# Strip attention on one Trainium2 core: eleven VectorE units in 14 of the 28 pairs instead of 21, and a new written-out order

## The chip, the core and the metric

The kernel runs on one core of one Trainium2 chip. A core has five engines that run their own instruction streams and meet only at semaphores: TensorE (PE; its weight loads are shown apart as PEld), VectorE (DVE), ScalarE (ACT), GpSimd (POOL) and SyncE (SP, which here only issues DMAs). The metric is device time in microseconds (us), smaller is better. Times of several runs are given as the median with the lowest and the highest; the profile is one further execution, with a time of its own.

## What is computed

A projection to q, k and v, attention inside strips, and an output projection, for an image of 224 x 224 tokens with 96 channels. The first 48 channels attend inside horizontal strips of 8 rows, the last 48 inside vertical strips of 8 columns; each strip has 8 x 224 = 1792 tokens.

```python
def reference(x, wqkv, wo):
    B, H, W, C = x.shape
    sw = 8
    C2 = C // 2
    nh, nw = (H // sw, W // sw)
    qkv = jnp.einsum('bhwc,cd->bhwd', x, wqkv)
    q, k, v = (qkv[..., :C].copy(), qkv[..., C:2 * C].copy(), qkv[..., 2 * C:].copy())
    scale = C2 ** (-0.5)
    qh = q[..., :C2].reshape(B * nh, sw * W, C2)
...
    ah = _softmax(jnp.einsum('bqc,bkc->bqk', qh, kh) * scale, axis=-1)
    oh = jnp.einsum('bqk,bkc->bqc', ah, vh).reshape(B, H, W, C2)
...
    return jnp.einsum('bhwc,cd->bhwd', o, wo)
```

## The kernel before

**Pairs, chunks and units.** 28 horizontal and 28 vertical strips are worked in pairs of two neighbours, `P` = 0 to 27: 0 to 13 are horizontal, 14 to 27 vertical. The 1792 queries of a pair come in four chunks (`CH`: 512, 512, 512 and 256). Keys come in 14 tiles of 128. One *unit* is 1024 columns of scores of the pair: a chunk of 512 queries against one tile of keys, for both strips, or the chunk of 256 queries against two tiles. So a pair has 14 + 14 + 14 + 7 = 49 units, and the kernel 1372.

**What a unit costs each engine.** PE makes the scores into two banks of PSUM (`qk_op`, L1015: 48 rows deep, the two strips in two row halves of the array). Then the exponential is taken, in one of two ways:

- on ACT (`add_a`, L1037): one ACTIVATE with Exp of 128 x 1024 from PSUM into a `PT` buffer; then PE makes one product with the values (`pv_op`, L968, 64 columns wide, the two strips in two column halves).
- on VectorE (`add_d`): L1075 reads the scores from PSUM and writes them as 16-bit integers, shifted so that the bits are a number's exponent and mantissa; L1088 and L1090 mask out mantissa (`U_sb`) and exponent (`E_sb`); L1094 multiplies I by U (`G_sb`). exp is E + G, and PE adds the two by making **two** value products. Two VectorE units share one L1088 and one L1090 of 2048 columns; an odd last unit of a pair has its own, of 1024 columns. The product of L1094 is made on POOL in two halves of 512, or on VectorE as one of 1024, as `PLAN["far"]` says (1 is POOL).

How many units of each chunk go to VectorE is in `NDC` and `NDP` (L25 to L30): 11 of 49 for pairs in `NDP`, 10 for the others. Before, `NDP` holds the 21 pairs with `P % 4 != 1`, so 21 x 11 + 7 x 10 = 301 units are VectorE's and 1071 are ACT's.

**Other work.** For the next pair, `prep` has PE make q, k (L686) and v (L761), VectorE move them out of PSUM (L700, L706, L766), and POOL centre k (L720, L724, L725). For a finished chunk VectorE copies the sums out (L931), PE applies `wo` (L809 for horizontal, L843 for vertical pairs, L847 at the end), and VectorE divides by the sum of the row (L796, L816, L853); in vertical pairs POOL adds the horizontal half (L859), and SP stores the result (L887).

**What sets the order.** The order is written out: `PLAN["pe"]`, `["dve"]` and `["pool"]` have one digit for each operation of these engines, in order, and the digit names the queue from which the next one is taken (`forced`). In `"pe"`, 1 and 2 are scores for ACT and for VectorE, 3 and 4 are value products of VectorE's and of ACT's units, 5 is the output projection, 6 the projections, 0 the start. In `"dve"`, 1 is L931, 2 is L1075, 3 the other moves out of PSUM, 4 is L1088, L1090 and L1094. ACT takes its exponentials one after the other in the order of the units. `PLAN["bank"]` gives the PSUM bank of each PE operation that opens one; a score result takes two of the eight. All engines run their streams strictly in that order, each instruction behind the semaphores of what it needs.

**Modes of PE.** Scores (L1015) and the vertical output projection (L843) use the array split by rows; all the rest uses it whole or split by columns. `SWITCH` in the planner charges each change between the two.

Of the kernel before, what the change touches and what calls it, by code (L numbers as in the profile page):

```python
# [25 lines left out]
NDP = {P: [3, 3, 3, 2] for P in range(28) if P % 4 != 1}  # L26


def ndc(P, c):
# [5 lines left out]
        "00000000000000000066611216162164144116444216331216431241641231431643441163446141541234133164412164412144312314"  # L35
        "31631451431244144126143153121433146124153341143444131235144123414414126413311463643164154134143163124614412614"
        "31145444134124163135164123135412144414412433112344144116344416312351431241641134445312416411463344144121543123"
        "14611364451231441163441233154113444412614412416312513411433444146123153114634413351541241634124136144123144116"
        "34434134124136134125144412316411463441213341146354154164144123133412314412414412316341163444135123164135414124"
        "41441461231634124133113644413312541441231641146344124313411634312441341261441231341441233144114644512316433153"  # L40
        "12416412314313411644431154444416415431531361241544123164114634114453341541231641241634125144144124133114434412"
        "54144113336412461441164431245143126134114533441414612351331241641146343124414411363412531441134464126134125144"
        "12413313412341541441163533416124415312461341144431163444412134412416313361441241541241631146441132331544113444"
        "12641441261331231341145444415412316311463433125144123164114534412341641146334144125413413312416441241641136441"
        "12444133113644312416441215431341241344123144164133123161331146345124153411444412361341134444615415416431313512"
        "44164123164114344412316311453441264134125144144124313312514414414611363354131254144123413416412416411463343141"
        "45124416313412416341241461113443344125144412133316412164412415411433334154124146134126133411634412441544121633"
        "11433544144164123154123146311446341241441164333125144113644512314314412441441612313412361341153444126133411263"
        "41441153444123416411463431333124154124163411264414411534441163354123164145123134412144414613312414312316441231"
        "44146135135312414414412613331163441144464451441331631241534124164114634114433441251344114644126314412514414123"  # L50
        "13412315411344436131641253144124163413514412416411463334143123146124134114644441214461133344125143411442154136"
        "12316412313313414412415441136446133125413124415411364441231544114634413313316441261341241641231441641144334125"
        "41341441231341241541241641146333134415413124414126133123154113644412315441146334154164144412613312316312464144"
        "11644341241334114634124415412415313613412413314364411444412531213314412313414313441241541163344143123154123154"
        "41146346114644611444463134151244415412316412416314412416411333441251344141153344412513341441241341241543164133"
        "14416412316312461441146443123144116336415312415314124413416412416412416412313313415441146341253134123154114464"
        "31244136144115343341431631241631241644126134114644412413311464441231334151244154124164124133113464431152344131"
        "34125134414412313415411463344154164164123163312416313464144126144144123153312414414412315312416411463331344164"
        "31441246144125144313412414414414615312361331231541136444412415411464441133644311344431531241531241641231641146"
        "44412413314441251334141125313341123444136144125144411463331463134125144412416411444334121641163363151244154124"  # L60
        "16312414316412164411433431231541144434415123315441231541144344123416411463341441246144121633113343412416441116"
        "36336124154124153124164134146124133124134134144415412415311633631541264431441254144134114334413441261331446121"
        "63414441231441126413311463441241541241531231614612431431331444144125143123314414412315441115336346113444641541"
        "64146163313613412414412614411344441231534124154124164114644412313412133411464441133633124415412315411344431251"
        "44411433441541241421316311366334166144164123134124144124154123153411466441313412441441231334154124153114444451"
        "312351331144444123313411434412541331241544113444124314311443152334154114421433114431433151534414445"),
    "dve": (
        "00000000000000000333333332332344323232443233313443432323244123443234323321342444133234423233333344133232333414"
        "23334323442322144313233244333233441323323333244312344323232344431323343133332342432344143232332344123443333332"
        "42421234413332344342333232144323323443214442323442424133321333244233344333331333233234431333323234243324124331"  # L70
        "32344323323344133323323444231323443323233244412334333132332443332144323233234431234432323244431333234312332344"
        "33233314423323234432144323423432412443123333244332344333333313323234412333234432321443233133323443232333413342"
        "32324431423443232324443134332312344323323344331323323443231233344234423321234431323234434323344132332323443313"
        "33234423442332124423133334423233443333132332344312333234421233244331332334432332334413232443231234432333234442"
        "41233431323323344323344413332323244314234423233234441344423132323344323344333313232323443214432332333444423144"
        "21244442343233441323323333334431333233234423231442313334234423233441343232334442133333423443232323444123343123"
        "32334443234441333323232344321444323323323214434441323234443233443331333234233442312344232332344344132314234442"
        "33332332334132334344441333233232344321444213323444323233443132332344432133333233244323234441233441332332344432"
        "34413232344432313332332334423324444412332313333323442344413423332444213234432332332334444421214423323333344333"
        "33333132234412332332344421234443132332344323441334232343333343242123323344334424412332313443432334442414423323"  # L80
        "34442144332343424444143333133333"),
    "pool": (
        "00000000022222221212122222222222222222112122222222222222221212122222222222222222221112222222222222222222211122"
        "22222222222222222121212222222222222222221212122222222222222222212112222222222222222222221212122222222222222222"
        "21212122222222222222222221112222222222222222222121212222222222222222222121212222222222222222222212121222222222"
        "22222222212121222222223223222232222121213222233332222322222121212222233322332232222333112122222222233223322331"
        "21213222232222332222121213222222333223222221211322222222333322222213131322223332222322222233321212123223222233"
        "2222222121212332232222223333221311222222332222222222212121232233332232222222222313112233322223333322333333"),
    "far": (
        "11111011110111111101111111111111111011111111110111011111111111111111101111111111111111111111111101111111111111"  # L90
        "11110111111111111111110111111111111111111111111110111011101100111111110010010111111010101101111001110111010111"
        "011110101100110110110111101101110111011100101101111111101011111011010100001000000"),
    "bank": (
        "76547012376502064256045260426402640264026046207420742047024702470240642053053205203520346034604163416416431463"
        "12356135375073057305730460247024602460406240640635046240260426013601376024072407240720420742706420462042604620"
        "43026402640261356035063503603650361356135631573173510357124571351753153153023520375137512642651365135713602460"
# [1127 lines left out]
```

## Time and profile before

| | before |
|---|---|
| median of 3 runs, us | 1007.16 (1005.09 to 1011.97) |
| profiled execution, us | 1004.3, of which its span is 1002.5 |
| granted TensorE clock | 0.999 |
| busy share PE, ACT, DVE, POOL | 99%, 99%, 94%, 68% |
| Exp ACTIVATEs on ACT | 1071 |
| L1075 on VectorE | 301 |
| L1094 on POOL, halves / on VectorE, whole | 482 / 60 |

In the profile a line names line of the program, engine, operation and tiles, then the count, busy time, mean length of one, and the idle time of the engine ahead of them with what ended it. Records of consecutive instructions of one engine can overlap, because an engine starts the next while the last is still draining; so the mean length of one is more than the distance from one start to the next, and a busy share of 99% doesn't say that an engine never waits: a short wait can vanish under the overlap. For ACT the distance between starts is the better measure.

### The profile page before, as it was taken

How to read it: one execution, taken by the hardware profiler on the slowest of the kernel's cores; microseconds unless marked ns; L12 is line 12 of the kernel's file. 1: busy time of each engine (PE TensorE's matmuls, PEld its weight loads, DVE VectorE, ACT ScalarE, POOL GpSimd, SP SyncE). 2: the span in 40 equal slices, each digit the busy share in tenths (PEclk: the TensorE clock that was granted, in tenths of full speed). 3: DMA queues.
4: the chain of work that ended last, by engine and by line, in shares of the span. 5: the costliest groups of instructions: out<-in, count | busy, mean ns of one | idle time of the engine just before them, and what ended most of it. 6: DMA issues, size and time to landing. Idle time of an engine off the chain costs nothing.

```text
span 1002.5 us, 24560 instructions
## 1 busy us (share of the span) xinstructions
PE 988.0 (99%) x10211; PEld 385.9 (38%) x10211; DVE 938.5 (94%) x1573; ACT 987.6 (99%) x1080; POOL 684.2 (68%) x660
## 2 busy tenths in 40 slices
PE   8999999999999999999999999999999999999997
PEld 3433433343343334334334333433433443343342
DVE  8999999999999999999899999999999999999997
ACT  7999999999999999999999999999999999999997
POOL 3676766667677676777776776776676777677652
PEclk9999999999999999999999999999999999999999
DMA  5102120220112023011111122222122221222012
GB/s 110 39 2 38 38 32 8 38 38 1 39 39 32 8 38 38 2 36 25 27 29 32 25 46 50 54 52 44 34 41 52 53 54 39 52 52 40 13 36 50
DMA packets 164712, 36.92 MB, mean 37 GB/s; under 512 B 164488, under 2 KB 164488, under 8 KB 164600
## 3 DMA queue, kind: packets, MB, share of 16 engines
q1 hardware_dynamic: 163016, 34.80, 18.5%
q8 instruction: 80, 1.31, 0.5%
q10 hardware_dynamic: 1584, 0.55, 0.2%
q14 instruction: 32, 0.26, 0.1%
HBM read 0.44 MB, written 9.63 MB: 10 GB/s over the span
## 4 chain that ended last, share of the span: by engine, by line
ACT 70%; PE 29%; DVE 1%; issue 0%
ACT PT L1037 70%; PE ps L968 13%; PE ps L1015 11%; PE ps L686 2%; PE ps L761 1%; PE ps L843 1%; PE ps L532 0%; PE ps L809 0%; DVE OT_sb L931 0%; PE ps L647 0%; DVE out_sb L866 0%; DVE I_sb L1075 0%; DVE E_sb L1090 0%; DVE U_sb L1088 0%; PE ps L679 0%
## 5 line engine op out<-in xcount | busy, mean ns | idle before, releaser
L1037 ACT ACTIVATE PT<-ps 128x1024 bf16<-128x1024 f32 x1071 | 983.5, 1119 | 2.9 <-PE ps L1015 1.5
L1094 POOL TENSOR_TENSOR G_sb<-I_sb,U_sb 128x512 bf16<-128x512 bf16 x482 | 544.0, 1153 | 250.7 <-DVE E_sb L1090 225.3
L1015 PE MATMUL ps<-QT_sb,KT_sb 48*128 48x512 bf16 (+1 forms) x3136 | 463.0, 356 | 4.7 <-ACT PT L1037 3.0
L1075 DVE TENSOR_SCALAR I_sb<-ps 128x1024 int16<-128x1024 f32 x301 | 367.3, 1220 | 24.6 <-PE ps L1015 21.1
L968 PE MATMUL ps<-PT,V_sb 128*64 128x512 bf16 (+1 forms) x2422 | 363.8, 363 | 1.1 <-ACT PT L1037 1.0
L1015 PEld LDWEIGHTS ps<-QT_sb,KT_sb 48*128 48x128 bf16 x3136 | 123.2, 93 | 307.4 <-ACT PT L1037 223.7
L968 PEld LDWEIGHTS ps<-PT,V_sb 128*64 128x64 bf16 x2422 | 119.2, 109 | 122.5 <-issue 94.9
L968 PE MATMUL ps<-G_sb,V_sb 128*64 128x512 bf16 (+1 forms) x714 | 115.6, 356 | 0.0
L968 PE MATMUL ps<-E_sb,V_sb 128*64 128x512 bf16 (+1 forms) x714 | 109.9, 356 | 0.6 <-DVE OT_sb L931 0.2
L1088 DVE TENSOR_SCALAR U_sb<-I_sb 128x2048 int16<-128x2048 int16 (+1 forms) x161 | 109.2, 678 | 0.2
L859 POOL TENSOR_TENSOR out_sb<-tmp,Ph_sb 128x480 bf16<-128x480 f32 (+1 forms) x84 | 84.9, 1026 | 30.0 <-DVE E_sb L1090 10.7
L1090 DVE TENSOR_SCALAR E_sb<-I_sb 128x2048 int16<-128x2048 int16 (+1 forms) x161 | 104.9, 652 | 0.2 <-PE ps L968 0.2
L686 PE MATMUL ps<-xT_sb,w_sb 96*64 96x512 bf16 (+1 forms) x444 | 77.6, 367 | 0.9 <-ACT PT L1037 0.5
L931 DVE CAST OT_sb<-ps 128x512 bf16<-128x512 f32 x112 | 69.3, 619 | 5.9 <-PE ps L968 5.0
L706 DVE TENSOR_SCALAR_CACHE_REDUCE KT_sb<-ps 128x512 bf16<-128x512 f32 x110 | 67.8, 620 | 7.4 <-PE ps L686 6.8
L700 DVE TENSOR_SCALAR QT_sb<-ps 128x512 bf16<-128x512 f32 (+1 forms) x111 | 68.1, 619 | 5.2 <-PE ps L686 4.1
L766 DVE CAST V_sb<-ps 128x480 bf16<-128x480 f32 (+2 forms) x85 | 51.7, 611 | 3.1 <-PE ps L761 2.8
L968 PEld LDWEIGHTS ps<-G_sb,V_sb 128*64 128x64 bf16 x714 | 36.4, 108 | 47.3 <-issue 28.8
L720 POOL TENSOR_SCALAR KT_sb<-KT_sb,negmean 128x1792 bf16<-128x1792 bf16 x27 | 47.5, 1759 | 10.3 <-DVE E_sb L1090 6.2
L816 DVE TENSOR_TENSOR Ph_sb<-ps,rc 128x480 bf16<-128x480 f32 (+1 forms) x84 | 52.2, 622 | 2.1
L853 DVE TENSOR_TENSOR tmp<-ps,rc 128x480 f32<-128x480 f32 (+1 forms) x84 | 51.9, 618 | 2.2
L968 PEld LDWEIGHTS ps<-E_sb,V_sb 128*64 128x64 bf16 x714 | 33.9, 108 | 43.1 <-issue 21.1
(47 smaller groups left out, 324.4 us busy)
## 6 DMA issues: line engine op xcount, KB each, us to landing
out_dram<-out_sb SPq DMA_DIRECT2D x208, 42.0 KB, 2.1
xT_sb<-in_x_dram SPq DMA_TRANSPOSE x251, 2.4
out_dram<-out_sb SPq DMA_DIRECT2D x22, 24.0 KB, 1.9
Ph_sb<-in_x_dram ACTq DMA_DIRECT2D x1, 336.0 KB, 3.0
out_dram<-out_sb ACTq DMA_DIRECT2D x6, 24.0 KB, 1.9
wo_sb<-in_wo_dram SPq DMA_DIRECT2D x4, 9.0 KB
wo_sb<-one_sb SPq DMA_DIRECT2D x4, 0.0 KB
w_sb<-in_wqkv_dram ACTq DMA_DIRECT2D x1, 54.0 KB, 4.6
```

The lines of the kernel that those rows point to most:

```text
L686: ins = e.matmul(bk[64 * w:64 * w + 64, 0:qs], lhsT=w_sb[0:C, wblk(P, kind), :], rhs=rhs, start=True, stop=True)
L700: return e.tensor_scalar(dst, src, QS, None, ALU.mult)
L706: return e.tensor_scalar(dst, src, 1.0, None, ALU.mult, ALU.add, accum_out=acc)
L859: return e.tensor_tensor(out_sb[b][:, k0:k0 + nk, ws[0], :], t, Ph_sb[:, k0:k0 + nk, j0 + ws[0], :], ALU.add)
L931: return e.tensor_copy(OT_sb[b][:, q0:q0 + qs], bk[:, 0:qs])
L968: return e.matmul(bank(k.bank)[64 * w:64 * w + 64, x0:x1], lhsT=lhs(w, kts[i])[p0:p1], rhs=rhs(w, i, qs)[p0:p1, x0:x1], start=(op.tok["fir ...
L1015: ins = e.matmul(bank(op.tok["s"][w])[:, i * qs:(i + 1) * qs], lhsT=KT_sb[b][64 * w:64 * w + C2, kt * 128:(kt + 1) * 128], rhs=QT_sb[b][64 ...
L1037: a.fn = lambda e: e.activation(PT[a.tok["p"]][:].rearrange("p (s n) -> p s n", s=2), two(q.tok["s"]), ACTF.Exp, scale=LN128)
L1075: return e.tensor_scalar(dst[:, at:at + 1024].rearrange("p (s n) -> p s n", s=2), two(src), 128.0 * ONE, 0.0, ALU.add, ALU.max)
L1088: f.fn = lambda e: e.tensor_scalar(U_sb[y()][:, 0:m], I_sb[y()][:, 0:m], M_FRAC, HALF, ALU.bitwise_and, ALU.bitwise_or)
L1090: x2.fn = lambda e: e.tensor_scalar(E_sb[x2.tok["l"]][:, 0:m], I_sb[y()][:, 0:m], M_EXP, E_LOW, ALU.bitwise_and, ALU.bitwise_or)
L1094: g.fn = lambda e: e.tensor_tensor(G_sb[x2.tok["l"]][:, i0:i1], I_sb[y()][:, i0:i1].bitcast(BF16), U_sb[y()][:, i0:i1].bitcast(BF16), ALU. ...
```

## The change

`NDP` now holds the 14 odd pairs. Pairs 0, 2, 4, ... 26 have 10 units on VectorE (in 4, 2, 2 and 2 of their chunks), the odd pairs 11 (3, 3, 3 and 2). Pairs with `P % 4` of 0 or 2 lose one unit to ACT (14 pairs), pairs with `P % 4` of 1 win one from it (7 pairs); those with 3 stay. In all 14 x 11 + 14 x 10 = 294 units are VectorE's and 1078 ACT's. The five written-out lists are all replaced by others:

```diff
-NDP = {P: [3, 3, 3, 2] for P in range(28) if P % 4 != 1}
+NDP = {P: [3, 3, 3, 2] for P in range(1,28,2)}
...
 PLAN = {
     "pe": (
-        "00000000000000000066611216162164144116444216331216431241641231431643441163446141541234133164412164412144312314"
...
+        "00000000000000000066111626162161441164444216331126431441261344144163136144123144614613412415413314612234141441"
...
     "far": (
-        "11111011110111111101111111111111111011111111110111011111111111111111101111111111111111111111111101111111111111"
...
+        "11111110111101111111111111111111101111111111111111111011111111111111111111111110111111111111110111111111111111"
```

What stands in the lists, counted:

| | before | after |
|---|---|---|
| scores for ACT / for VectorE in `"pe"` (1 / 2) | 1071 / 301 | 1078 / 294 |
| value products for ACT's / VectorE's units (4 / 3) | 1071 / 602 | 1078 / 588 |
| projections, output projections (6, 5) | 277, 169 | 277, 169 |
| changes of PE's mode, into rows and out of them together | 1783 | 1837 |
| L1088 and L1090 of 2048 / of 1024 columns, each | 140 / 21 | 140 / 14 |
| L1094 on POOL in halves / on VectorE | 482 / 60 | 482 / 53 |

The shapes of all instructions, the buffers, the DMAs and the code that follows the lists are the same. The order on PE, VectorE and POOL differs from the first pair on; ACT's order is the same but for seven more exponentials, and SP issues the same transfers with stores and loads interleaved a little differently. The last pair (27) has the same split as before.

More of the change, by code (lines that the diff above doesn't have):

```diff
@@ L39 @@
[L39 to L48, printed above, removed]
@@ new lines @@
+        "13463316412451441231341441233135124164134114463312541431241544113443124416411463334133161245134124164412613411"
+        "44446133154123164124135134412414414612413312331441146344124161233136154123154441331144446414116345441544131631"
+        "23514412316441163441143344125413411464412631441251441421313412315441134436135146412315412416341341412641441143"
+        "33441361531461231441246134124146144112335134114446412613312514412441331133444124154146412316133312614414451231"
+        "33114644415441631241441136334125144114634441164344133154124163114544412613412414413341241541231454113443163124"
@@ L112 @@
+        "54204620274027402740274074207542052045204520452450250725072450250270502506270627062706240624060246052602560256"
+        "056250620604270624042604024602303570350370350350173416416413461476040"),
 }
```

125 lines of the change are left out of this document (64 added, 61 removed).

## The prediction

> **What bounds the kernel now.** I read the page from the top: the busy shares, then the chain of waits, then the groups, and then I cut the span at the borders of the pairs.
>
> ```profile
> span 1002.5 us, 24560 instructions
> ...
> PE 988.0 (99%) x10211; PEld 385.9 (38%) x10211; DVE 938.5 (94%) x1573; ACT 987.6 (99%) x1080; POOL 684.2 (68%) x660
> ...
> ACT 70%; PE 29%; DVE 1%; issue 0%
> ...
> L1037 ACT ACTIVATE PT<-ps 128x1024 bf16<-128x1024 f32 x1071 | 983.5, 1119 | 2.9 <-PE ps L1015 1.5
> ```
>
> PE and ACT are both at 99%, and the chain that ended last runs over ACT for 70% of the span and over PE for 29%. ACT's share is one kind of instruction, the exponential of a unit, 1071 times. Visible idle time ahead of it is 2.9 us. The mean record of 1119 ns is no price: records overlap. The price is the distance between starts, and the view of one line's instructions gives the first and the last start:
>
> ```profile
> L1037 ACT ACTIVATE PT<-ps x1071: 1018/1116/1300, 9.9 to 994.4; 128x1024 bf16<-128x1024 f32 x179
> ...
>   PEld ps L1015: 223.7, 696
> ```
>
> (994.4 - 9.9) / 1070 steps = 0.920 us for one. The last row says who waited for the exponentials: 696 times PE stood with the weights of the next scores until ACT gave a bank back. So mostly PE, with its work at hand, is paced by ACT; where the chain changes to PE, it is the other way.
>
> The trace of before already holds both kinds of pair that the change trades in. Here are stretches from the first exponential of a pair to the first of the next one, busy time by engine: first seven pairs with 10 VectorE units and 39 exponentials (first, two others and sum), then nineteen with 11 units and 38 (the quickest, the three longest, and the sum; pairs 0 and 27 are left out for start and end). The counts in brackets take in one or two exponentials that run across a border.
>
> ```profile
> 45.24:81.48 36.24, 36.23 (x394) 14.19 (x392) 33.05 (x56) 36.08 (x40) 22.92 (x23) 1.00 0.21 40
> ...
> 607.28:643.55 36.27, 35.69 (x366) 14.71 (x363) 34.47 (x57) 35.84 (x40) 25.51 (x25) 1.00 0.29 58
> 748.97:784.61 35.64, 35.64 (x362) 14.24 (x361) 34.28 (x58) 35.64 (x40) 24.61 (x24) 1.00 0.26 52
> ...
> sum 251.18, PE 249.97 PEld 99.45 DVE 231.91 ACT 250.40 POOL 174.04; mean PE 35.71 PEld 14.21 DVE 33.13 ACT 35.77 POOL 24.86
> ```
>
> ```profile
> 537.23:571.94 34.71, 34.71 (x350) 13.84 (x350) 33.24 (x56) 34.71 (x39) 24.93 (x25) 1.00 0.13 27
> 571.94:607.28 35.34, 34.90 (x350) 13.78 (x348) 34.16 (x58) 35.18 (x39) 25.37 (x25) 1.00 0.23 46
> ...
> 713.30:748.97 35.67, 35.47 (x360) 13.83 (x355) 35.10 (x60) 35.13 (x39) 23.53 (x23) 1.00 0.23 46
> ...
> 854.36:889.82 35.46, 35.19 (x350) 13.47 (x348) 34.36 (x58) 35.12 (x39) 24.88 (x24) 1.00 0.27 54
> ...
> sum 664.13, PE 660.48 PEld 255.50 DVE 631.02 ACT 663.09 POOL 472.06; mean PE 34.76 PEld 13.45 DVE 33.21 ACT 34.90 POOL 24.85
> ```
>
> A pair of 39 takes 251.18 / 7 = 35.88 us, one of 38 takes 664.13 / 19 = 34.95: 0.920 us an exponential in both, so a pair is as long as its exponentials. The spread inside a kind (34.71 to 35.67) is what the order and the neighbours do; the longest of this kind are pairs 16, 20 and 24, where VectorE is busy for 97 to 98% of the stretch.
>
> **The change, part by part.**
>
> *ACT gets seven more exponentials.* A pair that goes from 38 to 39 is 35.88 - 34.95 = 0.93 us longer, one that goes back is as much shorter. Fourteen go one way, seven the other: 7 x 0.93 = **+6.5 us**. Nothing can hide it: ACT has no gap from 9.9 to 994.4 us into which they would fit (2.9 us of idle time in all).
>
> *VectorE loses seven whole units.* Rows of the operations that go:
>
> ```profile
> L1075 DVE TENSOR_SCALAR I_sb<-ps 128x1024 int16<-128x1024 f32 x301 | 367.3, 1220 | 24.6 <-PE ps L1015 21.1
> L1094 DVE TENSOR_TENSOR G_sb<-I_sb,U_sb 128x1024 bf16<-128x1024 bf16 x60 | 41.9, 707 | 0.1
> L1088 DVE TENSOR_SCALAR U_sb<-I_sb 128x1024 int16<-128x1024 int16 x21 | 9.3, 441 | 0.0
> L1090 DVE TENSOR_SCALAR E_sb<-I_sb 128x1024 int16<-128x1024 int16 x21 | 8.8, 419 | 0.0
> ```
>
> Per unit 1.220 + 0.441 + 0.419 + 0.707 = 2.79 us, for seven 19.5 us (the products on POOL stay 482, so those that go are VectorE's own). VectorE has 1% of the chain, so this is off the path: at nothing by itself. But it is what the three long pairs want, and 16, 20 and 24 are among those that lose a unit. The other sixteen of their kind take (664.13 - 106.47) / 16 = 34.85, so the three are 106.47 - 3 x 34.85 = 1.9 us too long. Against that, pairs 1 and 17, the two long ones of the other kind (36.24 and 36.27), now win a VectorE unit. I take half of it: **-1.0 us**; bounds 0 and -1.9.
>
> *PE loses seven value products and gains 54 changes of mode.* PE's steps can be read from a stretch of its timeline (start, length, instruction):
>
> ```profile
> 300.48 0.60 PE L968 MATMUL ps<-PT,V_sb 128*64 128x512 bf16 x4
> 301.01 0.61 PE L1015 MATMUL ps<-QT_sb,KT_sb 48*128 48x512 bf16 x4
> 301.55 0.41 PE L968 MATMUL ps<-E_sb,V_sb 128*64 128x512 bf16 x2
> 301.79 0.38 PE L968 MATMUL ps<-PT,V_sb 128*64 128x512 bf16 x2
> 302.11 0.39 PE L1015 MATMUL ps<-QT_sb,KT_sb 48*128 48x512 bf16 x2
> 302.43 0.41 PE L686 MATMUL ps<-xT_sb,w_sb 96*64 96x256 bf16 x4
> ```
>
> Two matmuls run side by side as one step. From a value product to the next in the same mode it is 301.79 - 301.55 = 0.24 us; from one to scores, 302.11 - 301.79 = 0.32; from scores back, 302.43 - 302.11 = 0.32; four scores take 301.55 - 301.01 = 0.54, so a step inside the mode is 0.22. A change of mode costs 0.08 to 0.10 us. The lists have 1783 changes before and 1837 after: 54 x 0.09 = +4.9, less 7 x 0.22 = 1.5 for the products, so PE's own work grows by 3.4 us. This is paid where PE sets the pace, by the chain 29% of the time, and covered by its waits for ACT elsewhere: 0.29 x 3.4 = **+1.0 us**; bounds 0, if all lies in those 223.7 us of waits, and +3.4, if that cover is gone.
>
> [...]
>
> *Start and end.* Pair 27 is split as before, and the end (8.1 us from the last start to the span's end, 1002.5 - 994.4) has the same chain. Pair 0 has four VectorE units in its first chunk instead of three; by the spread of single pairs above, up to 1 us either way, taken at nothing. SP issues the same transfers; the chain has no DMA in it.
>
> *Sum.* 6.5 - 1.0 + 1.0 = +6.5 us on the profiled execution's 1004.3 (span 1002.5 and 1.8 around it): **1010.8**. That execution was 2.9 us below the median of the three runs and 0.8 below the lowest, so a median may lie a little higher; I say **1011.5**.
>
> **The rivals.**
>
> *The new order gives the price back.* If every pair ran like the quickest of its kind in the rows above, the 28 would take 14 x 34.71 + 14 x 35.64 = 984.9 us, against 994.4 - 9.9 + 0.9 = 985.4 now: -0.5 us, a time of 1003.8. For it: seven units less on VectorE, which the long pairs want, and an order that alternates 10 and 11. Against it: nineteen pairs of 38 with one order that was laid out for them still average 0.24 above the quickest, and the added changes of mode go the other way. Between 1002 and 1007 us; chance 0.22.
>
> *Slower by more than the exponentials: PE becomes the late one.* Scores must be there before ACT has emptied its last pair of banks. In the quickest pair PE is already busy for 34.71 of 34.71 us. The extra changes are 27 into rows and 27 out, one round trip more in nearly every pair; where a round trip stands ahead of ACT's next scores and the banks ahead of it are used up, ACT waits for all of it. It decides from the point at which PE's work in a pair is longer than 34.95 or 35.88 us. PE's 3.4 us then count in full, and pairs stall as pair 20 does, 35.67 - 34.85 = 0.82 us; with half of the 28 so, nine more than the five long ones now, 9 x 0.82 = 7.4. 6.5 + 3.4 = 9.9 to 6.5 + 3.4 + 7.4 = 17.3 us: 1014 to 1022. For it: PE's 29% of the chain, and 54 changes more. Against it: seven value products less, and more time from ACT in 14 pairs. Chance 0.14.
>
> *A real gain.* Faster than the rows of the quickest pairs allow would need exponentials closer than 34.71 / 38 = 0.913 us apart; no pair shows that. Chance 0.02.
>
> That the change does not do what it says is ruled out by the counts of the lists.
>
> **How the numbers follow.** The forecast, with ACT paying for seven more exponentials, gets 0.62: its own range is 6.5 with the bounds above (-1.9 to 0, 0 to 3.4) and up to 2.9 for the runs, 1008 to 1015. The range for 8 in 10 reaches from 1004, into the order that gives it back, to 1018, into PE as the late one. A difference of about 1% is what a measurement of this kernel can tell from no change; around the median 1007.16 that is 997.1 to 1017.2. Faster: the last rival, 0.02, and scatter, together 0.03. Slower: the upper part of PE's case and a little of the forecast, with late medians, 0.12. The rest, 0.85, lies within.
>
> **What would show it.** In the profile after, the exponentials should count 1078, with 0.918 to 0.922 us between starts, and ACT still over 98%. Pairs with 39 should take about 35.9 us and with 38 about 34.95; pairs 16, 20 and 24 should be near 35.9, no longer half a microsecond and more above their kind. VectorE should be busy for about 919 us (938.5 - 19.5). ACT's share of the chain should stay at 70% or grow; if PE's share grows and the distance is over 0.925, the second rival holds, and if the distance falls under 0.916, the first. The prediction is wrong if the time between first and last exponential does not grow by about 7 x 0.92.

## The result, and the profile after

| | before | after |
|---|---|---|
| median of 20 runs, us | 1006.35 (1003.00 to 1011.97) | 1010.95 (1007.35 to 1014.03) |
| profiled execution, us | 1004.3 | 1010.55 |
| its span, us | 1002.5 | 1008.7 |
| its granted TensorE clock | 0.999 | 0.995 |

The ratio is 1.0041, 95% interval 1.0029 to 1.0052: slower by 0.4%, measurable over 20 runs, and inside the 1% that was called no change.

The page of the kernel after: span, busy shares, the chain that ended last by engine, and the group of the exponentials.

```profile
span 1008.7 us, 24514 instructions
...
PE 994.6 (99%) x10197; PEld 383.3 (38%) x10197; DVE 924.3 (92%) x1545; ACT 993.7 (99%) x1087; POOL 683.4 (68%) x660
...
ACT 94%; SPq 3%; PE 2%; DVE 0%; issue 0%; DMA 0%; DVEq 0%
...
L1037 ACT ACTIVATE PT<-ps 128x1024 bf16<-128x1024 f32 x1078 | 989.7, 1130 | 4.2 <-PE ps L1015 3.9
```

ACT's busy time grew by 993.7 - 987.6 = 6.1 us, PE's by 6.6, the span by 6.2. The chain now names ACT for 94% and PE for 2%; before it was 70 and 29. Read alone, that says that PE has room nearly everywhere; two experiments below show that it has not.

The view of the exponentials' line, after:

```profile
L1037 ACT ACTIVATE PT<-ps x1078: 1019/1129/1302, 9.3 to 1001.4; 128x1024 bf16<-128x1024 f32 x180
...
  PEld ps L1015: 229.9, 719
```

(1001.4 - 9.3) / 1077 = 0.921 us from one start to the next: the forecast distance. But not all of it is the price of an exponential, as a cut by pairs and, further down, the first pair show. First four of the thirteen pairs 2 to 26 with 39 exponentials (2, 16, 20, 24) with the sum of all thirteen, then two of the thirteen odd pairs with 38 (17, 19) with their sum. Columns as before: stretch, length, busy time of PE, PEld, DVE, ACT and POOL, granted clock, DMA share, GB/s.

```profile
83.63:119.62 35.99, 35.70 (x404) 13.94 (x404) 32.16 (x55) 35.76 (x40) 25.09 (x24) 1.00 0.22 40
...
578.23:614.01 35.78, 35.65 (x368) 14.06 (x364) 32.98 (x55) 35.78 (x41) 27.69 (x27) 1.00 0.16 33
...
719.98:755.80 35.82, 35.36 (x368) 14.30 (x365) 34.28 (x58) 35.82 (x41) 25.26 (x26) 1.00 0.26 52
...
861.06:897.02 35.96, 35.81 (x361) 14.08 (x359) 32.91 (x55) 35.96 (x40) 26.26 (x26) 1.00 0.27 53
...
sum 466.13, PE 462.90 PEld 182.27 DVE 425.10 ACT 465.88 POOL 328.78; mean PE 35.61 PEld 14.02 DVE 32.70 ACT 35.84 POOL 25.29
```

```profile
614.01:648.90 34.89, 34.86 (x345) 13.22 (x344) 32.55 (x55) 34.89 (x40) 24.87 (x25) 1.00 0.23 47
...
684.75:719.98 35.23, 34.42 (x337) 13.14 (x335) 32.26 (x53) 34.98 (x39) 25.58 (x26) 1.00 0.17 33
...
sum 452.66, PE 450.59 PEld 170.62 DVE 424.53 ACT 452.40 POOL 319.30; mean PE 34.66 PEld 13.12 DVE 32.66 ACT 34.80 POOL 24.56
```

A pair of 39 takes 466.13 / 13 = 35.86 us, one of 38 takes 452.66 / 13 = 34.82. The long pairs are gone: what stands out is pair 19, by 0.4 us. There PE waits for a load; the group of the projection to q and k names it (before, this idle time was 0.8 us and not put down to a DMA):

```profile
L686 PE MATMUL ps<-xT_sb,w_sb 96*64 96x512 bf16 x333 | 66.8, 395 | 1.6 <-DMA xT_sb<-in_x_dram 0.6 <-ACT xT_sb L652 0.4 <-DVE V_sb L766 0.2
```

Pair 19 differs from execution to execution (35.04 to 35.86 us in the profiles of this order without added PE work), while the others, behind pair 0, repeat to about 0.02 us where nothing in them was edited and the clock was full. So single pairs can be compared across profiles to a few hundredths.

What did not appear in the forecast is at the start. Two stretches of each kernel, first after, then before:

```profile
9.00:12.00 3.00, 2.72 (x29) 0.86 (x29) 2.85 (x5) 2.65 (x3) 0.00 (x0) 1.00 0.07 12
12.00:18.84 6.84, 6.58 (x28) 2.14 (x28) 4.60 (x8) 5.11 (x6) 2.54 (x3) 0.50 0.02 2
```

```profile
9.00:12.00 3.00, 2.01 (x25) 0.66 (x19) 2.93 (x8) 2.29 (x4) 0.00 (x0) 1.00 0.03 4
12.00:19.00 7.00, 6.69 (x56) 2.48 (x56) 6.72 (x12) 7.00 (x8) 2.61 (x3) 1.00 0.30 67
```

After, the granted clock is 0.50 from 12.00 to 18.84 us, PE makes 28 matmuls where it made 56 before, and ACT, with 5.11 us of 6.84, starves. It is 0.7% of the span, and neither the busy shares nor the chain point to it.

Pair 0 as a whole, first after, then before:

```profile
9.35:48.74 39.39, 38.69 (x357) 13.38 (x355) 34.33 (x55) 36.35 (x40) 21.58 (x21) 0.91 0.25 49
```

```profile
9.87:45.25 35.38, 33.83 (x342) 12.69 (x342) 34.39 (x56) 35.00 (x39) 20.87 (x20) 1.00 0.19 41
```

The whole span, cut once more (the last exponential is counted with 0.90 us):

| us | before | after | difference |
|---|---|---|---|
| up to the first exponential | 9.87 | 9.35 | -0.5 |
| pair 0 | 35.38 | 39.39 | +4.0 |
| pairs 1 to 27 | 950.05 | 953.53 | +3.5 |
| from there to the end | 7.21 | 6.44 | -0.8 |
| span | 1002.5 | 1008.7 | +6.2 |

The first and the last row move by this much between profiles of one order (the first exponential starts at 9.3 to 9.9 us in all of them), so they carry no finding.

### The profile page after: what moved, and what is told of

It is laid out like the page before. It is cut to its first block, busy times and chain, and to the rows that moved or that the text cites. A ratio compares the mean times of both kernels' runs of the same rounds, so it can differ in the third digit from the quotient of the medians.

```text
span 1008.7 us, 24514 instructions
## 1 busy us (share of the span) xinstructions
PE 994.6 (99%) x10197; PEld 383.3 (38%) x10197; DVE 924.3 (92%) x1545; ACT 993.7 (99%) x1087; POOL 683.4 (68%) x660
## 3 DMA queue, kind: packets, MB, share of 16 engines
q1 hardware_dynamic: 163016, 34.80, 18.3%
## 4 chain that ended last, share of the span: by engine, by line
ACT 94%; SPq 3%; PE 2%; DVE 0%; issue 0%; DMA 0%; DVEq 0%
ACT PT L1037 94%; SPq L558 2%; SPq L887 1%; PE ps L1015 1%; PE ps L968 1%; PE ps L532 0%; DMA xT_sb<-in_x_dram 0%; PE ps L686 0%; DVE KT_sb L706 0%; DVE out_sb L866 0%; PE ps L809 0%; PE ps L679 0%; ACT xT_sb L652 0%; PE ps L647 0%; DVE OT_sb L931 0%
## 5 line engine op out<-in xcount | busy, mean ns | idle before, releaser
L1037 ACT ACTIVATE PT<-ps 128x1024 bf16<-128x1024 f32 x1078 | 989.7, 1130 | 4.2 <-PE ps L1015 3.9
L1094 POOL TENSOR_TENSOR G_sb<-I_sb,U_sb 128x512 bf16<-128x512 bf16 x482 | 544.1, 1153 | 268.9 <-DVE E_sb L1090 251.5
L1015 PE MATMUL ps<-QT_sb,KT_sb 48*128 48x512 bf16 (+1 forms) x3136 | 468.0, 357 | 4.0 <-ACT PT L1037 1.2
L1075 DVE TENSOR_SCALAR I_sb<-ps 128x1024 int16<-128x1024 f32 x294 | 358.6, 1220 | 29.0 <-PE ps L1015 24.7
L968 PE MATMUL ps<-PT,V_sb 128*64 128x512 bf16 (+1 forms) x2436 | 372.2, 364 | 0.6 <-ACT PT L1037 0.6
L1015 PEld LDWEIGHTS ps<-QT_sb,KT_sb 48*128 48x128 bf16 x3136 | 123.7, 93 | 314.0 <-ACT PT L1037 229.9
L968 PE MATMUL ps<-G_sb,V_sb 128*64 128x512 bf16 (+1 forms) x700 | 113.0, 356 | 0.0
L1088 DVE TENSOR_SCALAR U_sb<-I_sb 128x2048 int16<-128x2048 int16 (+1 forms) x154 | 106.3, 690 | 0.2
L968 PE MATMUL ps<-E_sb,V_sb 128*64 128x512 bf16 (+1 forms) x700 | 104.8, 355 | 1.4 <-ACT PT L1037 0.4
L1090 DVE TENSOR_SCALAR E_sb<-I_sb 128x2048 int16<-128x2048 int16 (+1 forms) x154 | 101.9, 662 | 0.0
L686 PE MATMUL ps<-xT_sb,w_sb 96*64 96x512 bf16 (+1 forms) x444 | 78.1, 366 | 1.6 <-DMA xT_sb<-in_x_dram 0.6
```

The source lines that it names most:

```text
L686: ins = e.matmul(bk[64 * w:64 * w + 64, 0:qs], lhsT=w_sb[0:C, wblk(P, kind), :], rhs=rhs, start=True, stop=True)
L968: return e.matmul(bank(k.bank)[64 * w:64 * w + 64, x0:x1], lhsT=lhs(w, kts[i])[p0:p1], rhs=rhs(w, i, qs)[p0:p1, x0:x1], start=(op.tok["fir ...
L1015: ins = e.matmul(bank(op.tok["s"][w])[:, i * qs:(i + 1) * qs], lhsT=KT_sb[b][64 * w:64 * w + C2, kt * 128:(kt + 1) * 128], rhs=QT_sb[b][64 ...
L1037: a.fn = lambda e: e.activation(PT[a.tok["p"]][:].rearrange("p (s n) -> p s n", s=2), two(q.tok["s"]), ACTF.Exp, scale=LN128)
L1075: return e.tensor_scalar(dst[:, at:at + 1024].rearrange("p (s n) -> p s n", s=2), two(src), 128.0 * ONE, 0.0, ALU.add, ALU.max)
L1088: f.fn = lambda e: e.tensor_scalar(U_sb[y()][:, 0:m], I_sb[y()][:, 0:m], M_FRAC, HALF, ALU.bitwise_and, ALU.bitwise_or)
```

## Experiments

A session on a chip has its own runs of before, and each ratio, given with its 95% interval, is to those; it is worked out from all runs of both and not from the two medians, so it can differ from their quotient. In kernels with edits the lines after the edit shift by a few; the exponentials are named L1037, L1041, L1042 or L1043, the scores L1015 to L1021.

### What an exponential costs, and what is won by taking one away

Seven exponentials more in the kernel before, and nothing else:

```diff
-            a.fn = lambda e: e.activation(PT[...], two(q.tok["s"]), ACTF.Exp, scale=LN128)
+            def a_fn(e):
+                for out in ([junk[P // 4]] if i in TWICE else []) + [PT[a.tok["p"]]]:
+                    ins = e.activation(out..., two(q.tok["s"]), ACTF.Exp, scale=LN128)
+                return ins
```

> The kernel before, with seven exponentials made twice (one each in pairs 2, 6, ... 26; the extra result goes to a buffer that nobody reads). PE and VectorE have the same work in the same order. If ACT sets the pace, each extra exponential costs its step of 0.92 us: 7 x 0.92 = +6.4 us, ratio to before 1.0064, and each of the seven pairs is 0.9 us longer than in the profile before. If PE sets the pace for the 29% that the chain showed, 71% of it is seen: +4.6 us, 1.0046. If the order has room for it, nothing: 1.000.

Measured: 1010.54 us, before in the same session 1006.28; ratio 1.0031, 1.0007 to 1.0055. The sum over pairs 2, 6, 10, ... 26, by stretches, first before, then with the added exponentials:

```profile
sum 244.16, PE 242.39 PEld 94.44 DVE 232.11 ACT 244.16 POOL 170.52; mean PE 34.63 PEld 13.49 DVE 33.16 ACT 34.88 POOL 24.36
```

```profile
sum 250.54, PE 243.42 PEld 93.96 DVE 232.90 ACT 250.54 POOL 170.77; mean PE 34.77 PEld 13.42 DVE 33.27 ACT 35.79 POOL 24.40
```

250.54 - 244.16 = 6.4 us for seven: 0.91 us each, and the other pairs stay. An exponential added to a full ACT was paid here at the whole step. The medians differ by 4.3 us only, and the interval ends at 1.0055, below the 1.0064 of a full price. They mix in the granted clock, which differs from run to run: of the kernel with the added exponentials 6 of 12 runs had a mean clock of 0.998 or more, of before 8 of 35. The medians of these alone are 1009.51 and 1003.97 us, 5.5 us apart, and the lowest runs are 6.5 apart. The price rests on the stretches, where both clocks are 1.00. PE's busy time hardly changed (243.4 against 242.4), so the cost is ACT's alone.

The other way round, the kernel after with the seven exponentials that it won cut to 8 columns of each 512:

```diff
+                n = 8 if i in SHORT else 512
+                return e.activation(out[:, :, 0:n], at[:, :, 0:n], ACTF.Exp, scale=LN128)
```

> The changed kernel with seven exponentials (one each in pairs 2, 6, ... 26) cut from 512 to 8 columns per strip: most of these seven units' exponentials is left out. PE, VectorE and the order are the changed kernel's. If ACT's seven exponentials are what the change costs, this gives 7 x (0.92 - 0.2) = 5 us back (0.2 us is the record of the 128x8 ACTIVATE at the start): ratio to before 1.0041 - 0.0050 = 0.999. If PE's added changes of mode are the cost, the ratio stays at 1.004. If the start is the cost (the clock at half from 12.0 to 18.8 us), it still gives 5 us, but the pairs past the first are then shorter than before's by 3 us in sum.

Measured: 1008.38 us, ratio 1.0012, 0.9984 to 1.0040. The same seven pairs, first after, then with the cut:

```profile
sum 251.12, PE 249.01 PEld 97.89 DVE 229.59 ACT 250.87 POOL 174.62; mean PE 35.57 PEld 13.98 DVE 32.80 ACT 35.84 POOL 24.95
```

```profile
sum 250.31, PE 248.53 PEld 97.90 DVE 229.35 ACT 246.18 POOL 174.71; mean PE 35.50 PEld 13.99 DVE 32.76 ACT 35.17 POOL 24.96
```

ACT's busy time in them falls by 4.7 us, the pairs by 0.8. PE is busy for 248.53 of 250.31 us: it stands right behind ACT. So ACT and PE are late together in the kernel after, and what is taken from ACT alone is worth a sixth. The same cut was not made in the kernel before, so it isn't known whether ACT and PE were as close there. (That the median is lower by 1010.95 - 1008.38 = 2.6 us is mostly the start: in this profile the clock stayed at 1.00 there, and pair 0 took 36.60 us.)

### How much of added PE work is paid

A product of two columns, in the other mode, between two scores: one round trip of PE's mode each, in every ninth place where two score steps follow each other; 54 in the kernel before, 51 in the kernel after.

```diff
+                if last_mode[0] == "q":
+                    qq[0] += 1
+                    if qq[0] % 9 == 4:
+                        e.matmul(bank(op.tok["s"][0])[0:64, 0:2], lhsT=warm[:, 0:64], rhs=warm[:, 0:2], start=True, stop=True)
```

> The kernel before with 54 round trips of PE's mode more, spread evenly: ahead of a score step that follows a row-mode step, one matmul of two columns in the column mode (a constant tile) goes into the bank that the step then overwrites. PE's own work grows by 54 x 2 x 0.09 = 9.7 us, and 54 small matmuls; ACT, VectorE and the order are the same. By the share that I used (PE sets the pace for 29% of the time) +3 us, ratio 1.003. If PE's waits for ACT cover it, 1.000. If PE is as late as ACT nearly everywhere, most of it is paid: +7 to +10 us, 1.007 to 1.010. Pairs 1 to 27 took 950.05 us in the profile before; single pairs repeated to 0.02 us in other profiles, so this sum tells it best.

> The changed kernel with 51 round trips of PE's mode more in the same way: 51 x 2 x 0.09 = 9.2 us of PE's own work. Its chain runs over ACT for 94% and over PE for 2%. If that is a measure of PE's room, it costs less than 1 us in pairs 1 to 27 (953.53 us in the profile after). If PE stands just behind ACT, as the cut exponentials suggest (seven cut, 0.8 us won), it costs about as much as in the kernel before or more: 5 us and up, ratio to before 1.009.

Measured: in before 1011.48 us against 1005.23, ratio 1.0058 (1.0036 to 1.0079); in after 1014.68 (four runs), ratio to before 1.0087 (1.0058 to 1.0115). What one costs PE stands in the timeline of the second kernel (start, length, instruction; the added product is L1018):

```profile
301.49 0.39 PE L1021 MATMUL ps<-QT_sb,KT_sb 48*128 48x512 bf16 x2
301.82 0.19 PE L1018 MATMUL ps<-warm 128*64 128x2 bf16 x1
301.94 0.66 PE L1021 MATMUL ps<-QT_sb,KT_sb 48*128 48x512 bf16 x4
```

From score to score 301.94 - 301.49 = 0.45 us instead of 0.22: a round trip is 0.22 to 0.23 us, the two changes of the prediction (0.18) and a little for the product. What was paid, in stretches without the start, and in after without pair 19. Kernel before, pairs 13 to 27, without and with 29 round trips:

```profile
466.59:995.30 528.71, 524.56 (x5238) 206.06 (x5236) 503.73 (x838) 527.18 (x575) 363.15 (x349) 1.00 0.21 42
```

```profile
472.98:1004.38 531.40, 528.20 (x5265) 208.92 (x5263) 503.58 (x838) 529.11 (x575) 363.64 (x349) 1.00 0.21 41
```

2.7 us for 29 x 0.22 = 6.4: 0.42 of it. Kernel after, pairs 1 to 18 and 20 to 27, without and with 47:

```profile
48.74:684.75 636.01, 632.83 (x6674) 244.09 (x6672) 583.02 (x964) 635.76 (x694) 450.71 (x426) 1.00 0.16 30
...
719.98:1002.27 282.29, 280.51 (x2748) 108.51 (x2745) 266.76 (x445) 282.29 (x309) 183.41 (x179) 1.00 0.22 44
```

```profile
49.67:689.52 639.85, 637.62 (x6706) 248.25 (x6704) 584.20 (x964) 638.83 (x694) 451.21 (x426) 1.00 0.16 30
...
726.01:1009.64 283.63, 282.35 (x2763) 110.41 (x2760) 267.10 (x445) 283.41 (x309) 183.77 (x179) 1.00 0.23 44
```

3.84 + 1.34 = 5.2 us for 47 x 0.22 = 10.3: 0.50. The two shares are of different pairs. In pairs 20 to 27 alone, where both edited profiles ran at full clock, before pays 1.45 us (283.45 against 282.00) for 16 round trips and after the 1.34 us above for 15: 0.41 of the work in both. So the kernel whose chain gave PE 2% pays as much of added PE work as the one whose chain gave it 29%. The chain's share of an engine says through which instructions the last finish can be followed back; it doesn't measure the room of the others. (The first half of the profile of b_mode54 ran at a granted clock of 0.95 and is left out here; see the last section.)

### Is it VectorE that makes pairs long?

The kernel before, with VectorE's work on the odd last unit of the fourteen even pairs cut to 16 columns:

```diff
+            less = alone and j == 0 and P % 2 == 0
...
+                    n = 8 if less else 512
...
+            m_ = 16 if less else m
```

> The kernel before with the VectorE work of fourteen units (the odd last one of each even pair that has 11) cut to 16 columns: most of these fourteen units' L1075, L1088, L1090 and L1094 is left out, about 14 x 2 = 28 us of VectorE's work. ACT, PE, POOL and the order are the same. If VectorE's load is what makes pairs 16, 17, 20 and 24 long, they fall to 34.9 and 35.8 us, and pairs 1 to 27 from 950.05 to about 947.5 us: ratio 0.997. If the place of single steps in PE's order makes them long, they stay as they are to 0.1 us: ratio 1.000.

Measured: 1005.45 us against 1005.23, ratio 0.9995, 0.9974 to 1.0016. The page's busy shares, and by stretches pairs 16, 17, 20 and 24 of the edited kernel:

```profile
PE 986.2 (98%) x10211; PEld 384.1 (38%) x10211; DVE 918.2 (92%) x1573; ACT 987.5 (99%) x1080; POOL 685.6 (68%) x660
```

```profile
571.60:606.95 35.35, 34.91 (x350) 13.80 (x348) 33.15 (x58) 35.19 (x40) 25.92 (x26) 1.00 0.24 46
606.95:643.22 36.27, 35.69 (x367) 14.68 (x364) 34.04 (x56) 35.84 (x41) 25.00 (x25) 1.00 0.29 56
712.96:748.62 35.66, 35.46 (x360) 13.80 (x354) 33.61 (x61) 35.12 (x40) 23.64 (x24) 1.00 0.24 47
854.00:889.44 35.44, 35.17 (x350) 13.47 (x348) 33.54 (x59) 35.11 (x39) 24.91 (x24) 1.00 0.27 53
```

VectorE's busy time falls by 938.5 - 918.2 = 20.3 us, more than from before to after (938.5 - 924.3 = 14.2). In pair 20 it falls from 35.10 to 33.61 us, and the pair stays (35.67 and 35.66); 16 and 24 likewise. So the share of 97 to 98% for which VectorE is busy there does not make these pairs long. One thing this leaves open is a single VectorE step that comes late. The shortened units stand 28.0 to 28.4 us into these three pairs, and ACT's longest steps come earlier, at 20.8 us in pair 16, 20.7 in pair 20, 7.8 and 8.9 in pair 24; only the one at the end of pair 20, 35.7 us in, stands behind a shortened unit of its own pair, and it stays too (1.41 us from start to start before, 1.40 here).

The next suspect was the number of `PT` buffers: an exponential needs a free one, and PE's value products free them.

```diff
-    NPT, NY, NL, NR = 8, 3, 2, 4
+    NPT, NY, NL, NR = 12, 3, 2, 4
```

> The kernel before with 12 PT buffers instead of 8, nothing else (the written-out order of PE, VectorE and POOL is the same). In its trace six exponentials start 0.25 to 0.51 us late although their scores are there, each just behind a value product (592.75, 733.96, 748.97, 862.15, 863.30, 891.92 us; together 2.4 us): if they wait for a buffer that this product empties, more buffers take the waits away, pairs 16, 20 and 24 come down from 35.34, 35.67 and 35.46 to about 34.9, and pairs 1 to 27 from 950.05 to 947.7 to 948.2 us: ratio 0.998. If PE is behind anyway, the exponentials wait for their next scores instead and the sum stays within 0.5 us: ratio 1.000.

Measured: 1005.04 us against 1006.26, ratio 0.9986, 0.9968 to 1.0003. Pairs 20 and 21 of the edited kernel:

```profile
712.81:747.96 35.15, 34.94 (x356) 13.64 (x352) 34.57 (x60) 35.01 (x39) 23.34 (x23) 1.00 0.24 46
747.96:784.04 36.08, 36.08 (x368) 14.53 (x365) 34.83 (x58) 35.98 (x40) 24.86 (x25) 1.00 0.26 51
```

Pair 20 falls from 35.67 to 35.15, pair 21 rises from 35.64 to 36.08, in which PE is busy all the time; 16, 17 and 24 don't move, and pairs 1 to 27 together change by -0.1 us. So the buffers decide where a wait is seen, and hardly whether there is one.

### The start

The kernel after, with score steps 3 to 14 made twice, so that PE has more work from 9.8 to 19.9 us; then the same edit on the kernel before; and a smaller one on after, with score step 3 twice and 4 and 5 three times:

```diff
+                qk_n[0] += 1
+                for _ in range(2 if 3 <= qk_n[0] <= 14 else 1):
 -                for i, kt in enumerate(kts):
+                    for i, kt in enumerate(kts):
...
```

```diff
+                for _ in range({3: 2, 4: 3, 5: 3}.get(qk_n[0], 1)):
...
```

> The changed kernel with the third to the fourteenth score step of PE made twice (the same result into the same banks), so that PE is busier in the first 25 us. If the half clock from 12.0 to 18.8 us comes from PE doing too little there, the clock stays at 1.00, pair 0 takes about 36.5 us instead of 39.4, and the time falls by 2.5 to 3 us: ratio to before 1.0015, mean clock 0.999. If the clock falls whatever PE does, or if the lost time has another source, the ratio is 1.004 or, with 12 x 0.22 = 2.6 us of PE work more at the start, 1.0065.

> The kernel before with the same repeated score steps at the start. Its profile had the full clock at the start, but its runs spread from 1003 to 1012 us. If some of them lose time to a half clock at the start, the runs draw together near 1003 to 1005 and the ratio to before is about 0.998. If the spread has another source, the ratio is 1.000 to 1.002 and the runs spread as before.

> The changed kernel with fewer repeats at the start than in the earlier run: the third score step twice, the fourth and fifth three times, five repeats of 0.22 us = 1.1 us, where PE waits for ACT anyway. If the half clock in the changed kernel's start comes from too little PE work between 8.6 and 12 us, the clock holds in most runs, pair 0 takes 36.6 to 36.9 us, and the median falls by 2 to 3 us: ratio to before 1.001 to 1.002. If a clock that falls is a matter of when the kernel starts, whatever this work is, the ratio stays at 1.004.

Measured: a_head 1011.36 us (ratio 1.0041, 1.0016 to 1.0066), b_head 1006.79 (1.0001, 0.9977 to 1.0026), a_head2 1008.51 (1.0029, 1.0008 to 1.0051; before in its session 1005.23). In the profiles of a_head and a_head2 the clock stays at 1.00 throughout the start. In a_head the twelve repeats cost most of what they save: pair 0 takes 38.10 us, and b_head's 37.52 against 35.38 shows their price; the median is no lower than after's. In a_head2 they are few enough. Pair 0 and pairs 1 to 27 of a_head2:

```profile
9.54:46.36 36.82, 36.61 (x367) 13.05 (x365) 34.22 (x55) 35.99 (x39) 21.61 (x21) 1.00 0.26 52
46.36:1000.04 953.68, 947.76 (x9752) 365.66 (x9750) 881.83 (x1461) 953.02 (x1040) 660.55 (x627) 1.00 0.18 34
```

Pair 0 is 39.39 - 36.82 = 2.6 us shorter, the rest is unchanged (953.68 against 953.53), and 11 of 12 runs lie between 1008.0 and 1010.2 us. After's own 20 runs fall into the same two groups: four with a mean clock of 0.999 at 1007.4 to 1008.2 us, fourteen with 0.995 at 1010.2 to 1011.7 (and two with 0.994 above those). So in most runs of after the start costs some 2.5 to 3 us of half clock. (That the lower clock of those runs is lost at the start is seen in one profile of after (0.50 from 12.00 to 18.84 us) and in that of its edit with 51 products (0.52 from 13 to 16 us, 0.51 from 16 to 20); the other runs have no profile.)

### What a better version would be

Three attempts: after with twelve `PT` buffers and a_head2's start; before with twelve `PT` buffers, three score steps moved one or two places earlier in `PLAN["pe"]` (with the banks in `PLAN["bank"]` that go with them), and the second score step made four times; and before with this last edit alone.

```diff
+    NPT, NY, NL, NR = 12, 3, 2, 4
...
+                for _ in range({3: 2, 4: 3, 5: 3}.get(qk_n[0], 1)):
```

```diff
-        "...14412433112..."
+        "...14412413312..."
...
+                for _ in range({2: 4}.get(qk_n[0], 1)):
```

```diff
+                for _ in range({2: 4}.get(qk_n[0], 1)):
```

> The changed kernel with 12 PT buffers and with the start of the run before it (third score step twice, fourth and fifth three times). In the trace after, one exponential waits for a buffer (0.45 us at 92.25 us, pair 2). If the new order had no other wait of this kind, pair 2 falls from 35.99 to about 35.6, the other pairs stay, and the ratio to before is 1.0025 to 1.003. If seven more exponentials and PE's work fill the time anyway, nothing changes against the run before (pairs 1 to 27 at 953.5 us).

> The kernel before with 12 PT buffers, with three score steps moved ahead of two or one value products in PE's list where the trace shows ACT waiting for them with their banks free already (49.19, 80.57 and 608.88 us; waits of 0.33, 0.22 and 0.69 us), and with the second score step made four times, where PE waits for ACT at the start. If waits of ACT are what is left to win: buffers -2 us, moved steps -0.8 to -1.2 us, and fewer runs with a low clock at the start: pairs 1 to 27 at 947 us, ratio 0.996 to 0.997, faster than both kernels. If PE is the next one to be late, it stays at 0.999 to 1.000.

> The kernel before, with one thing changed: TensorE makes the second score step of the program four times over instead of once (the same four matmuls into the same banks, so the result is the same). In the profile of before TensorE stands for about 1 us there, so the repeats fill a gap and should move no exponential. Theory 'the run-to-run spread of before is set at the start too': in before's own runs a part lies 2 to 3 us above the lowest, the size of the stretch at half clock that after's profile shows; the gap filled, most runs should lie at the low end, the median 1003.8 to 1004.8, ratio 0.997 to 0.999, with the clock at 0.998 or more in most runs. Rival 'the spread comes from elsewhere' (the stall in pair 19, the chip as a whole): the median stays where that of before is in the same session, ratio 0.9995 to 1.001, with as many runs under a clock of 0.998 as before has. Under both the profile has the first pair at 35.3 to 35.5 us and pairs 1 to 27 at 950.0 to 950.1 us in sum, as before.

Measured: a_npt12h 1008.91 us (ratio 1.0041, 1.0018 to 1.0065), no better than a_head2; pair 2, expected at 35.6 us, falls only from 35.99 to 35.91. b_best 1004.85 (1.0000, 0.9981 to 1.0019): nine of twelve runs at 1004.1 to 1005.3, three at 1010 to 1012, and the moved scores made their pairs longer (pair 1: 36.24 to 36.56, pair 2: 34.80 to 35.04, pair 17: 36.27 to 36.50), so a local repair of the order takes more than it gives. b_head2 1005.09 against 1007.68, ratio 0.9974, 0.9950 to 0.9998: the one version whose interval lies below 1, and only just. Its session's 1007.68 is the highest of before's five medians (the others are 1005.23 to 1006.35), so that it beats before by a quarter of a percent isn't settled. The stretch that it fills, first before, then b_head2:

```profile
10.00:11.00 1.00, 0.04 (x2) 0.00 (x0) 1.00 (x2) 1.00 (x2) 0.00 (x0) 1.00 0.00 0
```

```profile
10.00:11.00 1.00, 0.65 (x8) 0.22 (x4) 1.00 (x3) 1.00 (x2) 0.00 (x0) 1.00 0.01 1
```

PE is busy for 0.65 us there instead of 0.04, no exponential moves (pair 0 takes 35.38 us in both), and outside pair 19, which waited 1.2 us longer for a load, pairs 1 to 27 agree to 0.01 us. The mean clock was 0.997 or more in 10 of its 12 runs, in 6 of the 17 of before. Over all sessions it was 0.998 or more in 32 of 109 runs of before, and in 18 of the 24 of b_head2 and b_best, which share this edit. The median of b_head2 lies 0.3 us above the band that was expected. That before, too, loses clock at its start in many runs fits this, but no profile of before shows it, since the one taken kept its clock: it stays an inference.

## Why the prediction was right, and where it was not

The time and the range held: 1011.5 forecast, 1010.95 measured. The terms held less well, and that the total came out is in part luck. Against the profiled span (+6.2 us; forecast +6.5; the medians of 20 runs differ by 4.6 only, since before's profile, which kept its clock, lies 2.0 us below its median and after's 0.4 below its own):

- **Seven exponentials, +6.5.** Right, and shown in isolation, in the kernel before: 6.4 us for seven.
- **VectorE's relief, -1.0.** Wrong in its mechanism. The three long pairs did come down to their kind, and 1 and 17 too; pairs 1 to 27 have six exponentials more, 6 x 0.91 = 5.5 us, and grew by 3.5, so the new order is worth 2.0 us net there. But 20 us less VectorE time in the old order was worth nothing. The step that failed was to take the busy share of 97 to 98% in pairs 16, 20 and 24 for the reason of their length.
- **PE's added changes of mode, +1.0.** The mechanism is right, the size too low. The share 0.29 was taken from the chain; measured it is 0.42 before and 0.50 after, which makes 1.4 to 1.7 of the 3.4 us. As this is inside the net 2.0, the new order must have won some 3.5 us elsewhere; that is a remainder, not a measurement.
- **Start and end, 0.** Wrong: 39.39 - 36.60 = 2.8 us of half clock (a_exp7cut leaves pair 0 as it is in after, and kept its clock there) and 36.60 - 35.38 - 0.91 = 0.3 of order in pair 0, less 1.3 by which the first exponential and the end came earlier in this profile. The bound of 1 us either way took no account of the clock.

So 6.4 - 2.0 + 2.8 + 0.3 - 1.3 = 6.2, and the total was right because two errors of opposite sign, 2.0 us of order and 1.8 of start and end, happened to cancel. Without losses of clock on either side the change costs about 4.3 us, two thirds of the price of its exponentials: the 11 runs of a_head2 with a mean clock of 0.998 or more have a median of 1008.46 us, the 9 such runs of before in its session 1004.21.

The forecast's own range does not follow from its bounds: 1004.3 with 6.5 - 1.9 = 4.6 at the least and 6.5 + 3.4 + 2.9 = 12.8 at the most is 1008.9 to 1017.1, not 1008 to 1015. The measured time lies in both.

**The rivals.** "The new order gives the price back" holds in part: 2.0 of 6.4 us net of PE's added work, and the long pairs are gone, which was its reason. "PE becomes the late one" did not come as a rise of pairs, but PE is about as late as ACT in the kernel after, as the cut exponentials show. "A real gain" stays out.

**The marks that were set.** 1078 exponentials, 0.921 us apart, pairs of 39 at 35.86, pairs 16, 20 and 24 at 35.78 to 35.96, ACT's share above 70%: as said. Pairs of 38 came out at 34.82 rather than 34.95. VectorE is busy for 924.3 us rather than 919. Its work did fall as reckoned: the lengths of all its records add up to 1032.6 us before and 1012.4 after, 20.2 less; they overlap less than before, so the busy time falls by 14.2 only. And the mark "time between first and last exponential grows by about 7 x 0.92" came near (992.0 - 984.5 = 7.5 us, against 6.4) although 2.8 of that was the clock: a mark over the whole span can't tell a price from a disturbance.

**What stays open.** What it is in the new order that removes the long pairs. VectorE's load as a whole and the number of `PT` buffers are excluded, a single late VectorE step is not; the likeliest is PE's sequence as a whole, since PE is what ACT waits for when it waits (4.1 of the 4.2 us ahead of the exponentials in after), and since three small moves in it changed the pairs that they touched. The old split with a new order, or the new split with the old one as far as it goes, was not tried.

## What to carry to other kernels

Where two engines are at 99%, cost an edit on each of them. Here work added to the pacing one was paid in full (0.91 us each at a step of 0.92, in the kernel before), work added to the other by 0.4 to 0.5, and work taken from the pacing one alone was worth a sixth (0.8 of 4.7 us, in the kernel after). Measure the second engine's room by adding a known amount of work to it, not by its share of the chain. Compare stretch by stretch, with the granted clock beside each, before a total is explained: here the total was right for reasons that were partly wrong.

## What the hardware showed unexpectedly

**Half a clock for 6.84 us without a real pause.** In after's profile PE was busy for 2.72 of the 3.00 us ahead of the drop; in before's it was busy for 2.01 of the same 3.00 and kept its clock. The granted clock was 1.00 from 9.00 to 12.00 us, 0.50 from there to 18.84 and 1.00 again up to 25; what sets these times was not shown. Which runs drop depends on more than the kernel: four of after's 20 ran at a mean clock of 0.999. PE stood still for 0.28 us in all of those 3 us, so no long pause was needed, and a few repeated matmuls went with a mean clock of 0.998 or more in 11 of a_head2's 12 runs.

In b_best's profile the same happened in pair 19, after a pause of PE of 1.73 us that ended at 683.98; three rows of its stretches:

```profile
683.00:684.80 1.80, 0.82 (x12) 0.57 (x14) 0.38 (x1) 0.74 (x1) 1.80 (x3) 1.00 0.28 57
684.80:686.00 1.20, 1.20 (x10) 0.57 (x9) 0.85 (x4) 0.61 (x1) 1.03 (x1) 0.51 0.22 44
...
692.00:695.00 3.00, 3.00 (x16) 0.87 (x14) 2.00 (x5) 1.77 (x2) 1.62 (x2) 0.50 0.22 47
```

The pair took 41.13 us instead of 34.93: a wait of under 2 us became 6. Nor does the length of the pause decide it: in the profile of a_mode51 PE stood for 1.7 us ahead of a projection (L686) in pair 19 too, and the clock stayed at 1.00.

**A clock of 0.95 on one core, for 470 us.** In the profile of b_mode54, in two of its stretches:

```profile
100.00:473.00 373.00, 372.86 (x4014) 144.88 (x4012) 343.29 (x567) 371.57 (x402) 262.89 (x246) 0.95 0.14 27
474.00:600.00 126.00, 125.40 (x1256) 49.16 (x1251) 115.92 (x196) 125.76 (x138) 90.24 (x86) 1.00 0.16 32
```

From 4 to 100 us the clock was 0.95 too. PE was busy for 372.86 of 373.00 us at 0.95 and for 125.40 of 126.00 at 1.00, so its busy time doesn't tell the two apart. The mean clock of this run was 0.975; of all runs on record one other, of the same kernel, had one as low (0.946). Its cause is open.
